# Loading the first rows per head pair, and ordering the first batch's steps by kind, in a fused attention and expert kernel

## The chip, the cores and the metric

The kernel runs on one core of one Trainium2 chip. The time is device microseconds of one execution. The kernel before was timed three times: 359.33, 359.04 and 358.71, median 359.04 us. One further execution was profiled.

In the text PE is TensorE (matmul, with PEld its weight load), DVE is VectorE, ACT is ScalarE, POOL is GpSimd, and SP is SyncE, which here only issues transfers.

## The reference

Attention over 4 batches, 8 heads, 768 positions, head size 64, with 4 sink positions and a window of 128; then a mixture of 4 experts over all 3072 tokens.

```python
scores = scale * q @ k.T
keep = (pos_k < 4) | (0 <= pos_q - pos_k < 128)
a = softmax(where(keep, scores, -1e9))
x = (a @ v) as [3072, 512]
p = domain_probs / domain_probs.sum(-1)
out = sum over e of p[:, e] * (relu(x @ w1[e]) @ w2[e])   # w1: 512x1024, w2: 1024x512
```

## The kernel before, in words

**Tiling.** A batch has 768 tokens, cut into three groups of 256 (g = 0, 1, 2; written (b, g)). Two heads make a head pair (hp 0 to 3), because two times 64 columns fill 128 partitions. For a group and a head pair the steps are: q and k rows are turned (`transposes`, lines 581 to 625, on TensorE for batch 0) and copied to `qkT`; `scores` (687 to 758) multiplies k by q into two PSUM banks, ScalarE takes the exponential into `aT` (line 746), VectorE multiplies the mask (line 754); `values` (763 to 830) multiplies by v, whose 65th column of ones gives the row sums, VectorE takes the reciprocal `R` (813) and multiplies (816, batch 0) or ScalarE does (825, later batches) into `onat`; `turn` (840 to 858) transposes that to `xT`, the input of the experts. In group 0 the mask is instead added on TensorE as a bias of -32768 before the scores (line 700). Groups 1 and 2 also use the sinks (`sinks`, 658), whose keys and values GpSimd prepares (lines 630 and 645).

**Experts.** For groups 0 and 1 of batch 0 the first layer of expert 0 is done directly (`emit_first`, line 1106, four pieces called hps of eight matmuls for a group and an expert), and so is that of (0, 2). Everything after, in `emit_fast` (1189, called cps), uses seven half-size products with sums of weights (`vf`, `qkn`, lines 404 to 410) and of tokens (`T`, line 1158) formed on VectorE. The second layer of groups (0, 0) and (0, 1) is direct (`emit_second`, 1433), of all others again in seven products (`emit_product`, 1358). Gates are applied in the first layer's eviction (lines 1223, 1131) from tiles that SP loads (485) out of a table in DRAM that `gates_by_row` writes (461 to 470).

**Transfers.** q and k of the first 256 rows of batch 0 come unconverted through SP and ScalarE's queue (`load_first`, 287) into `raw` tiles, and are converted by casts on VectorE and ScalarE (`cast_first`, 308). All other rows, v and the weights come through GpSimd, which converts in the transfer, one after the other in one queue: v blocks 0 and 1, then q and k rows of group 1 (`load_nat(0, 2)` and `(0, 3)`), v block 2, the first quarter of w1 of expert 0, v block 3, the other three quarters, w2 of expert 0 (lines 521 to 531), then what the loop adds.

**What sets the order.** Nothing is scheduled by the hardware: each engine runs its instructions in the order in which the program issues them. A planner at build time picks that order. It keeps a clock for each engine (`t`), adds an assumed duration for each instruction, and holds for every tile the time when it should be there. Its main loop (1494 to 1568) asks all possible TensorE steps for the time when they could run and a rank, and takes the lowest rank of those that are ready. Where nothing is ready for 220 ns it emits a filler product of 256 columns (`idle_products`, line 574). Work on ScalarE and VectorE is put on a list by `later(engine, ready, slack, run)`; when an engine's clock is free, `flush` takes, of the entries that are ready, the one with the smallest ready + slack. A small slack is thus a high rank. "any" lets the sooner of the two engines take it. The constants at the head of the kernel (60 to 113) are these ranks, shares and delays. `SHARE_OF` and `LEAD` pace the attention of the later batches against the experts' work, `GROW` is the earliest planner time (in ns) for `gates_by_row`.

Of the kernel before, what the change touches and what calls it, by code (L numbers as in the profile page):

```python
# [8 lines left out]
AF = mybir.ActivationFunctionType  # L9
# [7 lines left out]
def kernel(  # L17
# [20 lines left out]
    P = 128  # L38
# [19 lines left out]
    ]  # L58

    NGATE = 5  # L60
    START = {0: (1, 0), 1: (0, 1), 2: (0, 0), 3: (0, 0)}
    DENSE = 2
    NT3 = 3
    MIX = 4
    SHARE_OF = (0.634, 1.111, 1.102)
    LEAD = (1.272, 0.235)
    DUE = 0
    LOW_PRODUCT = 2.791
    LOW_SECOND = 4.402
    HIGH_PRODUCT = 0.207  # L70
    EARLY = 0.154
    GATE = 8921
    GATE0 = 5401
    FORM = 20576
    FORM2 = 37391
    TOKEN00 = 33179
    TOKEN0 = 1119
    WAIT2 = 16164
    WAIT1 = 5898
    LATE3 = 3  # L80
    TOKEN = 11155
    MARGIN = 494
    FULL = 7
    STEP0 = 0.141
    READY = 46
    WIDE = 2
    OPEN = 1.198
    ONACT = 1
    ONE = 2
    PAIR = 1  # L90
    SINK2 = 1
    PAD = 198
    MASKD = 99999999
    GROW = 24662
    ONLY2 = 1
    BEHIND = 7198
    CHORES = 2
    OWN = 2
    BIASED = 1
# [11 lines left out]
    FLIP = 421  # L111
    LATE = 259
    LATE1 = 12449

# [83 lines left out]
    def clock(engine, cols, rate=0.96, fixed=157):  # L198
        return act(cols) if engine == "act" else dve(cols, rate=rate, fixed=fixed)
# [86 lines left out]

    def load_first():

        raw = {name: mo.tile([P, 2, 4, 2 * D], FP32, name=f"{name}raw", tag=f"wide{i}", bufs=1) for i, name in enumerate("qk")}
        for half in range(2):  # L290
            hs = slice(4 * half, 4 * half + 4)
            for name, src in (("q", q), ("k", k)):
                x = raw[name][:, half]
                (nc.sync if name == "q" else nc.scalar).dma_start(
                    out=x, in_=src[0, hs, 0:G, :].rearrange("h (p t) d -> p h (t d)", t=2),
                )
                nat[0, half, name, "raw"] = x
            landed["first", half] = ((4870.0, 5180.0), (7550.0, 7350.0))[half]
            t["sp"] += 530

    def copy(engine, out, in_):
# [3 lines left out]
    qkn_free[-2:] = [1e12] * 2  # L305
    cast_at = {}

    def cast_first(half):
        hs = slice(4 * half, 4 * half + 4)

        def cast(at):
            cast_at[half] = at

        part = join(2, cast)
        for i, name in enumerate("qk"):
            def run(engine, i=i, name=name):
                copy(
                    engine, first[name][:, :, hs, :],
                    nat[0, half, name, "raw"].rearrange("p h (t d) -> p t h d", t=2),
                )  # L320
                part(clock(engine, 512))
            later(("dve", "act")[i], landed["first", half][i], 0, run)

    def rows_at(b, g):
        return max(landed.get(("qk", b, tb), 1e12) for tb in (2 * g, 2 * g + 1))
# [194 lines left out]
        pool(0, fixed=190)  # L520
    load_v(0, (0, 1))
    t["sw"] += 500
    for tb in (2, 3):
        load_nat(0, tb)
    load_v(0, (2,))
    load_w1(0, 4, [0])
    load_v(0, (3,))
    for i in range(1, 4):
        load_w1(0, 4, [i])
    t["sw"] += 700  # L530
    load_w2(0)

# [5 lines left out]
    low = [lent[:, 5 * P:8 * P], lent[:, 8 * P:10 * P]]  # L538
    nc.vector.tensor_scalar(
        out=low[0].rearrange("p (n q) -> p n q", n=3)[:, 0::2], in0=two, scalar1=LOW, scalar2=-LOW, op0=ALU.mult, op1=ALU.add,  # L540
    )
    nc.vector.tensor_scalar(out=low[0][:, P:2 * P], in0=own, scalar1=-LOW, scalar2=None, op0=ALU.mult)
    nc.vector.memset(low[0][0:NSINK, 0:2 * P], 0.0)
    nc.scalar.activation(out=low[1][:, 0:P], in_=own, func=AF.Copy, scale=-LOW)
    nc.scalar.activation(out=low[1][:, P:2 * P], in_=own, func=AF.Copy, scale=LOW, bias=-LOW)
    mask0 = consts.tile([P, 3 * P], BF16, name="mask0")
    mask1 = consts.tile([P, 2 * P], BF16, name="mask1")
    t["dve"] = t["act"] = 4600.0
    cast_first(0)
    flush(4700.0)  # L550
    for x in vx:
        nc.vector.memset(x[:, :, D:DX], 1.0)
    t["dve"] += 240.0
# [5 lines left out]
    nc.vector.memset(half, 0.0)  # L559
    for ph in range(2):  # L560
        nc.vector.memset(half[64 * ph:64 * ph + 64, ph:ph + 1], 1.0)
    for x in ksd:
        nc.vector.memset(x, 0.0)
    for x, y in zip((mask0, mask1), low):
        nc.vector.tensor_scalar(out=x, in0=y, scalar1=1 / LOW, scalar2=1.0, op0=ALU.mult, op1=ALU.add)
    t["dve"] += 400.0
    cast_first(1)

    acc = [psum.tile([P, 2 * G], FP32, name=f"acc{i}", tag=f"o{i}", bufs=1) for i in range(2)]

# [10 lines left out]
    def transposes(b, g, hp):  # L581

        if b not in qkT:
            qkT[b] = sb.tile([P, 2, NHP, S], BF16, name="qkT", tag="qkT", bufs=1)
        ready = max(cast_at[hp // 2] if (b, g) == (0, 0) else rows_at(b, g), free_at(2 if (b, g) == (0, 0) else 1))
# [6 lines left out]
        for i in range(2):  # L592
            for tt in range(2):
                if (b, g) == (0, 0):
                    nc.tensor.transpose(trs[i][:, i, tt], first["qk"[i]][:, tt, hs], ident)
                    continue
# [90 lines left out]
    def scores(b, hp, g, more=False):  # L687
# [4 lines left out]
        for ph in range(2):  # L692
# [4 lines left out]
        biased = b == 0 and g < BIASED  # L697
        if biased:
            for ph in range(2):
                nc.tensor.matmul(sps[ph][:, 0:w], lhsT=ident, rhs=low[min(g, 1)], start=True, stop=False, skip_group_check=True)  # L700
            pe(2 * w, ready, n=2)
        c = 0
        for (kb, qb, nq) in GROUPS[g]:
# [40 lines left out]
        for ph in range(2):  # L744
            def run(engine, ph=ph):
# [6 lines left out]
                def mask_one(engine):  # L752
                    x = a[:, ph].rearrange("p (n w) -> p n w", n=2)
                    nc.vector.tensor_mul(x, x, m[:, None, :].to_broadcast([P, 2, 2 * P]))
                    part(dve(w, rate=1.92))
                later("dve", at, 300, mask_one)
            later("act", done, 300 + 10 * ph, run)
        aTs[b, hp, g] = a

    def scores_ready(b, hp, g, n=1):  # L760
# [2 lines left out]
    def values(b, hp, g):  # L763
# [47 lines left out]
        def run(engine):  # L811
            R = sb.tile([P, 2, 2, 1], FP32, name="R", tag="R", bufs=6)
            nc.vector.reciprocal(out=R, in_=od[:, :, :, D:DX])  # L813
            at = dve(4, fixed=171)
            if b < ONACT:
                nc.vector.tensor_mul(  # L816
                    o[:, :, hp].rearrange("p q (h d) -> p q h d", h=2), od[:, :, :, 0:D], R.to_broadcast([P, 2, 2, D]),
                )
                scaled(dve(2 * P))
                return  # L820

            def multiply(engine):
# [17 lines left out]
    def turn(b, hp, g):  # L840
# [12 lines left out]
        def run(engine):  # L853
# [9 lines left out]
    class Attention:  # L863
# [23 lines left out]

        def flip_ready(self):
            _, b, g, hp = self.flips[0]
            rows = cast_at.get(hp // 2, 1e12) if (b, g) == (0, 0) else rows_at(b, g)  # L890
# [82 lines left out]
    class Mixture:  # L973


        def __init__(self):
            self.early = {g: list(range(E)) for g in range(DENSE)}
            self.open = []
            self.units = []
# [90 lines left out]
        def emit_first(self, what, ready):  # L1070
# [45 lines left out]
            if (b, g) not in PAIRS:  # L1116
                def run(engine):
# [343 lines left out]

    idle_products(acc[1], 9)
    mix = Mixture()
    att = Attention(0)
    work = [
# [137 lines left out]
```

## Time and profile before

| | |
|---|---|
| median of three runs | 359.04 us |
| profiled execution | 358.95 us, span 357.2 us, granted clock 1.00 |
| PE busy | 348.8 us, 98% |
| VectorE busy | 306.7 us, 86% |
| ScalarE busy | 168.7 us, 47% |
| GpSimd busy | 70.5 us, 20% |
| GpSimd's transfer queue | 17.31 MB, 55.4% of 16 transfer engines' span |

How to read it: the span runs from the first to the last instruction on the core. A line of a timeline or a chain gives start, duration, engine, source line, and written tile <- read tile. "[1.19 <-DMA kraw]" means that the engine sat idle for 1.19 us before it and that a transfer of kraw ended the wait. A busy share of PE is not work done: a matmul is pipelined, and its record holds its way through the array as well. Filler products count as busy.

### The profile page before, as it was taken

How to read it: one execution, taken by the hardware profiler on the slowest of the kernel's cores; microseconds unless marked ns; L12 is line 12 of the kernel's file. 1: busy time of each engine (PE TensorE's matmuls, PEld its weight loads, DVE VectorE, ACT ScalarE, POOL GpSimd, SP SyncE). 2: the span in 40 equal slices, each digit the busy share in tenths (PEclk: the TensorE clock that was granted, in tenths of full speed). 3: DMA queues.
4: the chain of work that ended last, by engine and by line, in shares of the span. 5: the costliest groups of instructions: out<-in, count | busy, mean ns of one | idle time of the engine just before them, and what ended most of it. 6: DMA issues, size and time to landing. Idle time of an engine off the chain costs nothing.

```text
span 357.2 us, 11108 instructions
## 1 busy us (share of the span) xinstructions
PE 348.8 (98%) x4673; PEld 302.6 (85%) x4673; DVE 306.7 (86%) x701; ACT 168.7 (47%) x432; POOL 70.5 (20%) x90
## 2 busy tenths in 40 slices
PE   8999999999999999999999999999999999999995
PEld 3675687777688998998998998899899999999884
DVE  6669999998799899899699799699799699999630
ACT  5866451437882922566444722926443632322110
POOL 8934114311260440420030620000000000000000
PEclk9999999999999999999999999999999999999999
DMA  9999999999993999691086999124112221100011
GB/s 175 185 195 203 230 210 174 137 135 139 227 148 42 138 168 157 75 119 46 32 68 111 148 156 139 50 54 55 44 32 63 59 52 51 37 31 31 1 61 60
DMA packets 115318, 37.86 MB, mean 106 GB/s; under 512 B 97196, under 2 KB 110764, under 8 KB 115268
## 3 DMA queue, kind: packets, MB, share of 16 engines
q0 software_dynamic: 74416, 17.31, 55.4%
q1 hardware_dynamic: 39796, 19.32, 29.3%
q8 instruction: 36, 0.59, 0.7%
q10 hardware_dynamic: 1056, 0.52, 0.6%
q14 instruction: 14, 0.11, 0.1%
HBM read 41.03 MB, written 6.34 MB: 133 GB/s over the span
## 4 chain that ended last, share of the span: by engine, by line
PE 83%; DVE 6%; ACT 5%; DMA 2%; issue 1%; POOL 1%; DVEq 0%
PE cps L1189 35%; PE acc L1358 31%; PE acc L1433 7%; PE hps L1106 3%; PE sps L706 3%; ACT onat L825 2%; PE od L786 2%; ACT aT L746 2%; DMA vx<-in_v_dram 2%; DVE H L1223 1%; DVE cps L1239 1%; DMA gates<-gate_rows 1%; PE od L779 1%; DVE onat L816 1%; DVE H L1254 1%
## 5 line engine op out<-in xcount | busy, mean ns | idle before, releaser
L1189 PEld LDWEIGHTS <-w 128*128 128x128 bf16 x1408 | 87.1, 98 | 3.5 <-issue 1.0
L1358 PEld LDWEIGHTS <-H 128*128 128x128 bf16 x720 | 66.6, 98 | 7.9 <-issue 1.2
L1223 DVE SCALAR_TENSOR_TENSOR H<-cps,gates 128x512 bf16<-128x512 f32 x105 | 69.8, 683 | 0.0
L1358 PE MATMUL acc<-w,H 128*128 128x256 bf16 x432 | 56.8, 273 | 0.1
L1189 PE MATMUL cps<-xT,w 128*128 128x128 bf16 x704 | 52.5, 219 | 0.5 <-ACT onat L825 0.5
L1189 PE MATMUL cps<-T,w 128*128 128x128 bf16 x704 | 52.5, 219 | 0.1
L746 ACT ACTIVATE aT<-sps 128x512 bf16<-128x512 f32 (+1 forms) x96 | 46.5, 571 | 9.7 <-PE sps L706 9.5
L1232 ACT COPY cps<-cps 128x512 f32<-128x512 f32 x44 | 25.7, 592 | 44.2 <-PE cps L1189 33.8
L1405 ACT COPY osb<-acc 128x256 f32<-128x256 f32 x40 | 15.4, 384 | 59.2 <-PE acc L1358 59.2
L825 ACT ACTIVATE onat<-od,R 128x64 bf16<-128x64 f32 x144 | 32.8, 349 | 21.7 <-DVE R L813 21.7
L1358 PE MATMUL acc<-wf,H 128*128 128x256 bf16 x288 | 39.3, 273 | 0.0
L1189 PEld LDWEIGHTS <-qkn 128*128 128x128 bf16 x576 | 34.8, 98 | 1.1 <-issue 0.2
L1239 DVE TENSOR_TENSOR cps<-H,cps 128x512 f32<-128x512 f32 x40 | 27.7, 691 | 9.0 <-PE cps L1189 6.2
L1358 PEld LDWEIGHTS <-S 128*128 128x128 bf16 x320 | 30.2, 98 | 4.2 <-issue 1.0
L1245 ACT COPY H<-cps 128x512 f32<-128x512 f32 x40 | 23.7, 600 | 18.1 <-PE cps L1189 18.1
L1433 PE MATMUL acc<-w,H 128*128 128x512 bf16 x128 | 30.1, 379 | 0.0
L1189 PEld LDWEIGHTS <-vf 128*128 128x128 bf16 x480 | 28.8, 98 | 0.1
L331 POOL DMA_DIRECT2D vx<-in_v_dram x24 | 21.4, 909 | 37.4 <-PE od L786 25.9
L1254 DVE TENSOR_TENSOR H<-H,cps 128x512 f32<-128x512 f32 x40 | 27.0, 680 | 1.7 <-PE cps L1189 1.6
L271 POOL DMA_DIRECT2D rows<-in_q_dram x18 | 16.0, 887 | 61.1 <-DMA qkT<-rows 51.0
L1189 PE MATMUL cps<-T,qkn 128*128 128x128 bf16 x384 | 27.3, 219 | 0.1
L727 DVE TENSOR_TENSOR aT<-aT,mask 128x1024 bf16<-128x1024 bf16 (+1 forms) x36 | 22.8, 641 | 1.9 <-ACT aT L746 1.6
(123 smaller groups left out, 524.2 us busy)
## 6 DMA issues: line engine op xcount, KB each, us to landing
w<-in_moe_w_dram POOLq DMA_DIRECT2D x7, 1024.0 KB, 23.1
out_dram<-osb SPq DMA_DIRECT2D x23, 256.0 KB
gates<-gate_rows SPq DMA_DIRECT2D x40, 128.0 KB
vx<-in_v_dram POOLq DMA_DIRECT2D x24, 128.0 KB, 10.0
rows<-in_q_dram POOLq DMA_DIRECT2D x18, 128.0 KB, 6.4
rows<-in_k_dram POOLq DMA_DIRECT2D x18, 128.0 KB, 6.7
w<-in_moe_w_dram POOLq DMA_DIRECT2D x4, 256.0 KB, 8.4
kraw<-in_k_dram ACTq DMA_DIRECT2D x2, 256.0 KB
```

The costliest lines, as they stand in the source:

```text
L331: nc.gpsimd.dma_start(out=vx[tb][:, :, 0:D], in_=v[b, :, tb * P:(tb + 1) * P, :].rearrange("h p d -> p h d"),)
L727: nc.vector.tensor_mul(x, x, m[:, None, :].to_broadcast([P, n, 2 * w // n]))
L746: nc.scalar.activation(out=a[:, ph], in_=sps[ph][:, 0:w], func=AF.Exp, scale=scale)
L825: nc.scalar.mul(o[:, qi, hp, ph * D:(ph + 1) * D], od[:, qi, ph, 0:D], R[:, qi, ph])
L1189: nc.tensor.matmul(y[:, f], lhsT=A[:, d, f * P:(f + 1) * P], rhs=T[:, d], start=(m in ("P1", "P5") and f == 0 and d == 0), stop=(d == 1), ...
L1223: nc.vector.scalar_tensor_tensor(out=dst, in0=src, scalar=0.0, in1=gate, op0=ALU.max, op1=ALU.mult)
L1232: nc.scalar.copy(out=tiles["Y"], in_=y)
L1239: nc.vector.tensor_add(tiles["V"], c5, tiles["X"])
L1245: nc.scalar.copy(out=c5, in_=y)
L1254: nc.vector.tensor_add(c5, c5, y)
L1358: nc.tensor.matmul(x, lhsT=self.operand(b, g, e, m)[:, f], rhs=forms[e][m][:, f], start=(k == 0 and f == 0 and m in (("P1", "P5", "P2") if ...
L1433: nc.tensor.matmul(op, lhsT=H[:, fb // QF, fb % QF, s], rhs=w2_sb[e][:, fb, :], start=(fb == 0), stop=(fb == NFB - 1),)
```

## The change: what it does

1. The first rows of q and k are loaded per head pair (four transfers of 128 KB each) instead of per four heads (two of 256 KB). k of head pairs 0 to 2 goes on ScalarE's queue, the other five on SP's. They are cast per head pair: k of pairs 0 and 1 on ScalarE, the other six on VectorE.
2. GpSimd's queue takes group 1's k rows before its q rows, and the first quarter of w1 of expert 0 before v block 2.
3. In batch 0, the slack of each kind of step is a constant of its own: exponentials 562, masks 1574, reciprocals 1728, turn copies 2154, evictions of hps 221 (the first eight with an engine given by a list), normalisation on ScalarE 269. Before they were 300, 300, 500, 200 and 400. Normalisation of head pairs 0 and 3 of group 0 and head pair 0 of group 1 moves to ScalarE.
4. Clearing and mask instructions of VectorE at the start go on the planner's list. The second mask is made from `own` in two instructions instead of from a second bias tile, which is dropped with its two ScalarE instructions.
5. Nine fillers of 512 columns at the start become four. Many constants of the planner have other values, `GROW` among them (24662 becomes 35000).

```diff
-    SHARE_OF = (0.634, 1.111, 1.102)
-    LEAD = (1.272, 0.235)
+    SHARE_OF = (0.61, 1.111, 1.102)
+    LEAD = (1.272, 0.328)
...
-    GROW = 24662
+    GROW = 35000
...
+    FIRST = (3500.0, 4500.0, 5500.0, 7200.0)
+    CAST = (("dve", "act"), ("dve", "act"), ("dve", "dve"), ("dve", "dve"))
+    BEGIN = (3450.0, 3600.0)
+    CLEAR = 1000
+    EARLY0 = (("n", 3), ("n", 2), ("w", 0), ("v", 2), ("v", 3), ("w", 1), ("w", 2), ("w", 3))
+    ACT0 = (0, 3)
+    ACT1 = (0,)
+    HPS0 = ("dve", "act", "any", "any", "dve", "dve", "act", "any")
+    S_MASK = 1574
+    S_VAL = 1728
+    S_TURN = 2154
+    S_HPS = 221
+    S_EXP = 562
+    S_MUL = 269
+    NACT = 3
+    NIDLE = 4
...
-        for half in range(2):
-            hs = slice(4 * half, 4 * half + 4)
+        for hp in range(NHP):
             for name, src in (("q", q), ("k", k)):
-                x = raw[name][:, half]
-                (nc.sync if name == "q" else nc.scalar).dma_start(
+                x = raw[name][:, hp]
+                (nc.scalar if name == "k" and hp < NACT else nc.sync).dma_start(
...
-                part(clock(engine, 512))
-            later(("dve", "act")[i], landed["first", half][i], 0, run)
+                part(clock(engine, 256))
+            later(CAST[hp][i], FIRST[hp], 100 * hp, run)
...
-    for tb in (2, 3):
-        load_nat(0, tb)
-    load_v(0, (2,))
-    load_w1(0, 4, [0])
-    load_v(0, (3,))
-    for i in range(1, 4):
-        load_w1(0, 4, [i])
+    for kind, i in EARLY0:
...
-    nc.scalar.activation(out=low[1][:, 0:P], in_=own, func=AF.Copy, scale=-LOW)
-    nc.scalar.activation(out=low[1][:, P:2 * P], in_=own, func=AF.Copy, scale=LOW, bias=-LOW)
...
+        nc.vector.tensor_scalar(out=mask1[:, 0:P], in0=own, scalar1=-1.0, scalar2=1.0, op0=ALU.mult, op1=ALU.add)
+        nc.vector.tensor_copy(out=mask1[:, P:2 * P], in_=own)
...
-                later("dve", at, 300, mask_one)
-            later("act", done, 300 + 10 * ph, run)
+                later("dve", at, S_MASK, mask_one)
+            later("act", done, (300 if b else S_EXP) + 10 * ph, run)
...
-            if b < ONACT:
+            if b < ONACT and hp not in ((ACT0, ACT1, ())[g]):
...
-            later("act", at, 600, multiply)
-        later("dve", done, 500, run)
+            later("act", at, 600 if b else S_MUL, multiply)
+        later("dve", done, 500 if b else S_VAL, run)
...
-        later("any", done, 200, run)
+        later("any", done, S_TURN, run)
...
-                later("any", end, 400, run)
+                later(HPS0[self.nhps] if self.nhps < len(HPS0) else "any", end, S_HPS, run)
+                self.nhps += 1
...
-    idle_products(acc[1], 9)
+    idle_products(acc[1], NIDLE)
```

More of the change, by code (lines that the diff above doesn't have):

```diff
@@ L60 @@
     NGATE = 5
+    FIRST = (3500.0, 4500.0, 5500.0, 7200.0)
[3 more added lines that the diff above has]
+    EARLY0 = (("n", 3), ("n", 2), ("w", 0), ("v", 2), ("v", 3), ("w", 1), ("w", 2), ("w", 3))
+    BIAS1 = ()
+    ACT0 = (0, 3)
[9 more added lines that the diff above has]
+    NIDLE = 4
     START = {0: (1, 0), 1: (0, 1), 2: (0, 0), 3: (0, 0)}
@@ L64 @@
     MIX = 4
-    SHARE_OF = (0.634, 1.111, 1.102)
-    LEAD = (1.272, 0.235)
+    SHARE_OF = (0.61, 1.111, 1.102)
+    LEAD = (1.272, 0.328)
     DUE = 0
[L68 to L79, printed above, removed]
+    LOW_PRODUCT = 2.872
+    LOW_SECOND = 4.475
+    HIGH_PRODUCT = 0
+    EARLY = 0.272
+    GATE = 9087
+    GATE0 = 5108
+    FORM = 22227
+    FORM2 = 45355
+    TOKEN00 = 28000
+    TOKEN0 = 1500
+    WAIT2 = 16819
+    WAIT1 = 5930
     LATE3 = 3
-    TOKEN = 11155
-    MARGIN = 494
+    TOKEN = 12447
+    MARGIN = 500
     FULL = 7
-    STEP0 = 0.141
-    READY = 46
+    STEP0 = 0.281
+    READY = 200
     WIDE = 2
-    OPEN = 1.198
+    OPEN = 0.991
     ONACT = 1
@@ L93 @@
     MASKD = 99999999
-    GROW = 24662
+    GROW = 35000
     ONLY2 = 1
-    BEHIND = 7198
+    BEHIND = 7891
     CHORES = 2
@@ L110 @@
     WARM = 6600.0
-    FLIP = 421
+    FLIP = 200
     LATE = 259
@@ L287, in load_first @@
     def load_first():
-        raw = {name: mo.tile([P, 2, 4, 2 * D], FP32, name=f"{name}raw", tag=f"wide{i}", bufs=1) for i, name in enumerate("qk")}
-        for half in range(2):
-            hs = slice(4 * half, 4 * half + 4)
+        raw = {name: mo.tile([P, NHP, 4 * D], FP32, name=f"{name}raw", tag=f"wide{i}", bufs=1) for i, name in enumerate("qk")}
+        for hp in range(NHP):
             for name, src in (("q", q), ("k", k)):
-                x = raw[name][:, half]
-                (nc.sync if name == "q" else nc.scalar).dma_start(
-                    out=x, in_=src[0, hs, 0:G, :].rearrange("h (p t) d -> p h (t d)", t=2),
-                )
-                nat[0, half, name, "raw"] = x
-            landed["first", half] = ((4870.0, 5180.0), (7550.0, 7350.0))[half]
+                x = raw[name][:, hp]
+                (nc.scalar if name == "k" and hp < NACT else nc.sync).dma_start(
+                    out=x.rearrange("p (h c) -> p h c", h=2),
+                    in_=src[0, 2 * hp:2 * hp + 2, 0:G, :].rearrange("h (p t) d -> p h (t d)", t=2),
+                )
+                nat[0, hp, name, "raw"] = x
             t["sp"] += 530
@@ L306, with cast_first, run @@
     cast_at = {}
-    def cast_first(half):
-        hs = slice(4 * half, 4 * half + 4)
+    def cast_first(hp):
         def cast(at):
-            cast_at[half] = at
+            cast_at[hp] = at
         part = join(2, cast)
         for i, name in enumerate("qk"):
-            def run(engine, i=i, name=name):
+            def run(engine, name=name):
                 copy(
-                    engine, first[name][:, :, hs, :],
-                    nat[0, half, name, "raw"].rearrange("p h (t d) -> p t h d", t=2),
-                )
-                part(clock(engine, 512))
-            later(("dve", "act")[i], landed["first", half][i], 0, run)
+                    engine, first[name][:, :, 2 * hp:2 * hp + 2],
+                    nat[0, hp, name, "raw"].rearrange("p (h t d) -> p t h d", h=2, t=2),
+                )
+                part(clock(engine, 256))
+            later(CAST[hp][i], FIRST[hp], 100 * hp, run)
     def rows_at(b, g):
@@ L522 @@
     t["sw"] += 500
-    for tb in (2, 3):
-        load_nat(0, tb)
-    load_v(0, (2,))
-    load_w1(0, 4, [0])
-    load_v(0, (3,))
-    for i in range(1, 4):
-        load_w1(0, 4, [i])
+    for kind, i in EARLY0:
+        if kind == "n":
+            load_nat(0, i)
+        elif kind == "v":
+            load_v(0, (i,))
+        else:
+            load_w1(0, 4, [i])
     t["sw"] += 700
@@ L537 @@
     LOW = 32768.0
-    low = [lent[:, 5 * P:8 * P], lent[:, 8 * P:10 * P]]
+    low = lent[:, 5 * P:8 * P]
     nc.vector.tensor_scalar(
-        out=low[0].rearrange("p (n q) -> p n q", n=3)[:, 0::2], in0=two, scalar1=LOW, scalar2=-LOW, op0=ALU.mult, op1=ALU.add,
+        out=low.rearrange("p (n q) -> p n q", n=3)[:, 0::2], in0=two, scalar1=LOW, scalar2=-LOW, op0=ALU.mult, op1=ALU.add,
     )
-    nc.vector.tensor_scalar(out=low[0][:, P:2 * P], in0=own, scalar1=-LOW, scalar2=None, op0=ALU.mult)
-    nc.vector.memset(low[0][0:NSINK, 0:2 * P], 0.0)
-    nc.scalar.activation(out=low[1][:, 0:P], in_=own, func=AF.Copy, scale=-LOW)
-    nc.scalar.activation(out=low[1][:, P:2 * P], in_=own, func=AF.Copy, scale=LOW, bias=-LOW)
+    nc.vector.tensor_scalar(out=low[:, P:2 * P], in0=own, scalar1=-LOW, scalar2=None, op0=ALU.mult)
+    if BIAS1:
+        low1 = lent[:, 8 * P:10 * P]
+        nc.vector.tensor_copy(out=low1[:, 0:P], in_=low[:, P:2 * P])
+        nc.vector.tensor_copy(out=low1[:, P:2 * P], in_=low[:, 2 * P:3 * P])
+    nc.vector.memset(low[0:NSINK, 0:2 * P], 0.0)
     mask0 = consts.tile([P, 3 * P], BF16, name="mask0")
     mask1 = consts.tile([P, 2 * P], BF16, name="mask1")
-    t["dve"] = t["act"] = 4600.0
-    cast_first(0)
-    flush(4700.0)
     for x in vx:
         nc.vector.memset(x[:, :, D:DX], 1.0)
-    t["dve"] += 240.0
     vsd = {}
@@ L557, with clear, masks @@
     ksd = [consts.tile([P, NHP, 32], BF16, name=f"ksd{i}") for i in range(2)]
[L559 to L567, printed above, removed]
+    t["dve"], t["act"] = BEGIN
+    for hp in range(NHP):
+        cast_first(hp)
+    def clear(engine):
+        nc.vector.memset(half, 0.0)
+        for ph in range(2):
+            nc.vector.memset(half[64 * ph:64 * ph + 64, ph:ph + 1], 1.0)
+        for x in ksd:
+            nc.vector.memset(x, 0.0)
+        t["dve"] += 400.0
+    def masks(engine):
+        nc.vector.tensor_scalar(out=mask0, in0=low, scalar1=1 / LOW, scalar2=1.0, op0=ALU.mult, op1=ALU.add)
+        nc.vector.tensor_scalar(out=mask1[:, 0:P], in0=own, scalar1=-1.0, scalar2=1.0, op0=ALU.mult, op1=ALU.add)
+        nc.vector.tensor_copy(out=mask1[:, P:2 * P], in_=own)
+        t["dve"] += 500.0
+    later("dve", 3600.0, CLEAR, clear)
+    later("dve", 3600.0, CLEAR + 300, masks)
     acc = [psum.tile([P, 2 * G], FP32, name=f"acc{i}", tag=f"o{i}", bufs=1) for i in range(2)]
@@ L584, in transposes @@
             qkT[b] = sb.tile([P, 2, NHP, S], BF16, name="qkT", tag="qkT", bufs=1)
-        ready = max(cast_at[hp // 2] if (b, g) == (0, 0) else rows_at(b, g), free_at(2 if (b, g) == (0, 0) else 1))
+        ready = max(cast_at[hp] if (b, g) == (0, 0) else rows_at(b, g), free_at(2 if (b, g) == (0, 0) else 1))
         slots, trs = [], []
@@ L592, in transposes @@
         for i in range(2):
+            if (b, g) == (0, 0):
+                for tt in range(2):
+                    nc.tensor.transpose(trs[i][:, i, tt], first["qk"[i]][:, tt, hs], ident)
+                continue
             for tt in range(2):
-                if (b, g) == (0, 0):
-                    nc.tensor.transpose(trs[i][:, i, tt], first["qk"[i]][:, tt, hs], ident)
-                    continue
                 for ph in range(2):
@@ L696, in scores @@
             ring[i] = 1e12
-        biased = b == 0 and g < BIASED
+        biased = b == 0 and (g < BIASED or g == 1 and hp in BIAS1)
         if biased:
             for ph in range(2):
-                nc.tensor.matmul(sps[ph][:, 0:w], lhsT=ident, rhs=low[min(g, 1)], start=True, stop=False, skip_group_check=True)
+                nc.tensor.matmul(
+                    sps[ph][:, 0:w].rearrange("p (n w) -> p n w", w=3 * P if g == 0 else 2 * P), lhsT=ident,
+                    rhs=low[:, None, :] if g == 0 else low1[:, None, :].to_broadcast([P, 2, 2 * P]),
+                    start=True, stop=False, skip_group_check=True,
+                )
             pe(2 * w, ready, n=2)
@@ L889, in flip_ready @@
             _, b, g, hp = self.flips[0]
-            rows = cast_at.get(hp // 2, 1e12) if (b, g) == (0, 0) else rows_at(b, g)
+            rows = cast_at.get(hp, 1e12) if (b, g) == (0, 0) else rows_at(b, g)
             return max(rows, free_at(2 if (b, g) == (0, 0) else 1), scored_at.get(b - 1, 0.0))
@@ L976, in __init__ @@
         def __init__(self):
+            self.nhps = 0
             self.early = {g: list(range(E)) for g in range(DENSE)}
```

## The prediction

> **What bounds the kernel now.** I read the page's busy totals first, then the busy time by stage, then the chain that ended last over the first 60 us, then the landings of the early transfers. TensorE (PE) is called 98% busy, but a matmul's record holds its pipeline latency, so I counted work instead: 104 matmuls of 128 columns take 5.81 us in the chain, 55.9 ns each, and eight of 512 columns take 1.73 us, 216 ns each. Both are columns / 2.4 GHz + 2.5 ns. Summed that way over all matmuls (a pair that uses 64 rows each counted once, four that use 32 columns each counted once, the filler products of line 574 left out) the useful work is 338 us. The span is 357.2, so 19 us are not work, and I placed them with the same sum over windows: 5.0 us from 0 to 5, 2.5 from 5 to 10, 1.5 from 10 to 13, 1.1 from 13 to 20, 1.1 from 20 to 25, 1.1 from 25 to 33: 12.3 in all before 33 us. From 33 to 354 only 3.6 are lost (2.2 of them between 80 and 120), and the end takes 3.7. So the kernel is bound by TensorE work after 33 us, and by the start before it. This change is mostly in the start.
>
> The busy time by stage; columns are busy time of PE, weight load, VectorE (DVE), ScalarE (ACT), GpSimd (POOL), granted clock, DMA share and GB/s:
>
> ```profile
> 5.00:10.00 5.00, 4.56 (x47) 2.57 (x45) 2.32 (x7) 3.88 (x10) 5.00 (x7) 1.00 1.97 193
> 20.00:25.00 5.00, 4.15 (x53) 3.41 (x50) 3.58 (x14) 2.54 (x5) 0.51 (x1) 1.00 1.42 199
> 30.00:40.00 10.00, 9.73 (x116) 5.88 (x111) 9.54 (x29) 6.49 (x14) 2.03 (x3) 1.00 1.20 219
> 40.00:50.00 10.00, 10.00 (x113) 7.83 (x112) 9.11 (x17) 5.09 (x10) 1.75 (x2) 1.00 1.17 218
> 60.00:80.00 20.00, 19.93 (x263) 15.93 (x261) 19.90 (x37) 8.85 (x16) 6.95 (x8) 1.00 1.81 140
> 100.00:120.00 20.00, 19.25 (x286) 17.24 (x284) 19.86 (x52) 11.64 (x37) 3.99 (x5) 1.00 1.11 90
> ```
>
> The reader should see a PE that has room until 25 us, and a VectorE that is nearly full from 30 us on. The chain, over the start:
>
> ```profile
> 3.52 5.80 DMA vx<-in_v_dram
> 12.03 0.55 PE acc L574 x5
> 15.22 1.58 ACT aT L746 x3
> 22.77 0.30 PE tx L847 x2
> 23.09 0.38 ACT xT L302
> 23.52 2.45 PE hps L1106 x21
> 25.97 0.60 PE acc L956 x4
> 31.33 1.83 PE acc L1433 x8
> ```
>
> The first thing the kernel waits for at length is not q or k but the second block of v, landed at 3.52 + 5.80 = 9.32. Then filler at 12.03, then group 1's exponentials and normalisation up to 23.46, then three first-layer pieces (hps), then the second layer (line 1433). The transfers issued by GpSimd go through one queue in order; issue plus time to landing, the first of these lines issued at 7.11 and the second at 10.94:
>
> ```profile
> w<-in_moe_w_dram POOLq DMA_DIRECT2D x1, 256.0 KB, 7.5
> w<-in_moe_w_dram POOLq DMA_DIRECT2D x1, 1024.0 KB, 14.0
> ```
>
> So expert 0's first quarter of w1 lands at 14.6 and its w2 at 24.9. In the same way group 1's q rows land at 10.4, its k rows at 12.1, v block 2 at 13.2, v block 3 at 15.5, the other quarters at 16.7, 18.4 and 19.5. Last, the first rows:
>
> ```profile
> 4.48 0.43 DVE L302 CAST qkn<-qraw 128x512 bf16<-128x512 f32 x1
> 4.93 0.62 ACT L302 CAST qkn<-kraw 128x512 bf16<-128x512 f32 x1 [1.19 <-DMA kraw<-in_k_dram]
> 5.72 0.54 PEld L595 LDWEIGHTS <-qkn 128*128 128x128 bf16 x8
> ```
>
> The first transposes come 0.17 us after ScalarE's cast ends, and that cast waited for k.
>
> **First rows per head pair.** The bytes stay; four transfers of 128 KB replace two of 256 KB per tensor. Counting packets of ScalarE's queue in half microseconds (16, 144, 244, 124, 74, 213, 232 from 2.5 to 6.0), its first 528 packets, one 256 KB transfer with its completions, are through at 4.5; the cast began 0.43 later. Half of them, 264, are through at about 3.7, so k of head pair 0 can be cast at about 4.15. A ScalarE copy of 128x256 takes 0.37 to 0.41 here; half the present cast is 0.31; I take 0.40, and 4.15 + 0.40 + 0.17 puts the first transposes at 4.7, 1.0 earlier. Head pair 2 follows at about 6.4 instead of 7.77 (third transfer through near 5.45). Head pair 3 needs all bytes (done at 6.1, plus 0.43) and two VectorE casts: 7.4 to 8.0 instead of 8.12. One more k transfer on SP, and two more q, push SP's v-sink loads back by three issues of 0.5 us; GpSimd uses them at 13.92, so that is covered unless they slip by more than 5 us. A third issue on ScalarE puts its table load 0.55 later (1.94 to 2.5, end 3.8), still before 4.15; the two bias activations it loses (0.31 and 0.29) had waited for nothing. VectorE makes the second mask in two instructions (0.15 to 0.25 each) where it had half of a 0.71 pair: at most 0.2, in a stretch where it was idle 1.23 us.
>
> The Trainium skill, page "DMA: Bandwidth & Descriptors", section "Anatomy of one DMA", gives a SWDGE fit of about 2.0 us plus bytes/436 GB/s; these are not SWDGE transfers, but by it halving one saves an estimated 0.3 us only, k could be cast at 4.65, and the sum would be 358.2, 0.5 of the 1.2 being lost. The packets counted above decide for 4.15 and for 357.7.
>
> **What covers it.** Values need v at 9.32, and GpSimd's order ahead of it is untouched. So the second or so gained at the front is not gained at 9.32. What is gained is that the softmax of head pairs 2 and 3 is no longer behind it: today their exponentials end at 11.11 and 12.32. Then ScalarE's two casts (0.8), four copies (1.4) and eight exponentials (8 x 0.43 = 3.5) from 4.15 are 5.7, so 9.9; with head pair 3's transposes at 7.8, copies 0.65, scores 0.7 and two exponentials 0.9 it is 10.1 to 10.5. One normalisation moved to ScalarE ahead of them (four instructions, 0.84) makes it at most 11.3. Normalising the four pairs on two engines (VectorE 0.6 each, ScalarE 0.84 each) and one turn each (0.3 and 0.38) then ends group 0 near 13.1 against 14.32: 1.2 earlier.
>
> **First quarter of the weights ahead of v block 2.** One 128 KB v block is worth 1.1 us of the queue (12.1 to 13.2). So the quarter lands near 13.5, not 14.6, and v block 2 at 14.6. Values of group 1 need block 3 (15.5, unmoved), so block 2 costs nothing. Swapping q and k rows changes nothing either, both are needed.
>
> **Steps ordered by kind, and the second cap.** Group 1's transposes start at 13.00 and its k rows are there at 12.1: 0.9 of room, more if the order on ScalarE (full from 14 to 18) or VectorE (full from 18 to 22) gets better: one normalisation less on VectorE is 0.42, and first-layer evictions now ranked ahead free banks sooner. Lower bound 0.9 from the k rows if nothing gets shorter, none at all if the chain only swaps waits. Upper bound: w2 of expert 0 at 24.9. The three hps and the gate transposes end at 26.49 now, so no more than 1.5 can be won before PE has nothing left to do until 24.9. I take 1.2, what group 0 gains, nearer the upper end since 2.2 us of PE time are still idle between 13 and 25.
>
> **Does it stay.** From 33 to 80 PE loses nothing in the trace, and it kept four dense pieces of expert 0 (3.5 us, at 52 to 58) in hand, so a PE that comes 1.2 us early to 34.9 (w1 of expert 1) and 41.7 (its w2) has other work. The gate-row sums move from 22.63, idle VectorE, to 35 or later: 0.24 + 0.18 + 0.30 + 0.32 = 1.04 us in its full stretch. PE loses nothing there now, so I cost it at nothing; 1.04 is its upper bound. The renumbered ranks and paces reorder everything after 33. No row prices that: at best it takes back part of the 3.6 us lost there, at worst it loses as much again. I take zero, since nothing in the rows leans either way. The filler cut from nine to four costs nothing by itself: single fillers are still put in wherever a wait is foreseen.
>
> **Sum.** The profiled execution took 358.95 for a span of 357.2, 1.7 outside it, 0.1 below the median of 359.04. 358.95 - 1.2 = 357.75; I say 357.7.
>
> **Rivals.** *Hidden:* group 1's chain is bound by eight exponentials of 0.52 and VectorE's eight masks of 0.43 and four normalisations of 0.6, whatever comes before; then its last turn stays near 23.1 and nothing is won: 358.9. For it: ScalarE is busy 4.0 of 4.0 us from 14 to 18. Against: it starts only at 13.00 with data there at 12.1. Chance 0.10.
>
> *Cold array:* 512-column fillers follow each other by 0.43 us up to 5.2, twice the later pitch, so the array runs at half rate for the first four microseconds although the rows grant 1.00. With fewer fillers and a gap near 4.2 this could last to about 8.5. The work of group 0 up to the scores is 0.9 + 1.3 + 0.9 = 3.1 us at full rate, 6.2 at half: from 4.7 it ends at 10.9, not 9.4, and 0.9 of the 1.2 is lost: 358.6. Chance 0.05. The Trainium skill, "TensorE: Matmul & The Clock Gate", section "What's actually happening", says that it takes about 3.4 us of sustained activity in a free-running window; the trace's switch near 5.4, 4.0 after the first filler, agrees.
>
> *Slower, by the pacing of later batches:* attention of batch 1 runs beside expert work from 80 to 120 and costs 2.2 us there, with ScalarE's normalisations and exponentials in the chain (98.48 to 101.95, 120.90 to 123.4). Batches 2 and 3 lose 0.9 (160 to 200) and 0.7 (220 to 240). The new shares call batch 1's steps due 4% sooner, so more of them meet unready scores or a full VectorE. If each of the later two loses what batch 1 loses, that adds 1.3 + 1.5 = 2.8: 358.95 - 1.2 + 2.8 = 360.5. It decides when the loss after 33 us passes 3.6 + 1.2 + 0.7 = 5.5. For it: the present order loses only 1% there, so a new one has more ways down than up. Chance 0.28.
>
> **How the numbers follow.** Forecast 0.57, hidden 0.10, cold 0.05, slower 0.28. A measurement can tell about 0.2%, 0.7 us. The forecast's own range is 356.5 (1.5 won at the start and 1.0 of the 3.6 later) to 358.3. The time falls below 356.4 perhaps once in fourteen (a larger part of the 3.6), and the slower case reaches beyond 361 as often. So 356.4 to 361.0. Faster 0.57; same 0.15, hidden and cold; slower 0.28.
>
> **What would show it.** Right: first transposes at 4.5 to 5.0, all exponentials of group 0 by 11.3, the first hps by 14, group 1's last turn by 22.5, then either no gap or a short wait for w2 at 24.9, useful work at 33 us about 1.2 ahead. Wrong: first values of group 0 much later than 9.4, or a loss after 33 us above 5.

## The result, and the profile after

The changed kernel takes 360.44 us (median of 7, 359.72 to 362.76) against 358.80 for the kernel before (7 runs, 358.70 to 359.33): 1.0052 times as long, 95% interval 1.0029 to 1.0076. It was forecast to be faster, at 357.7. The profiled execution took 359.72 for a span of 358.0. It is the fastest of the seven, so what the others lose beyond it, 0.7 us at the median, is not in this trace.

PE's busy total is unchanged (348.8 us in both). The time by stage of the changed kernel, columns as in the prediction:

```profile
20.00:25.00 5.00, 4.94 (x57) 4.27 (x55) 3.52 (x11) 2.32 (x6) 1.35 (x2) 1.00 1.38 200
40.00:50.00 10.00, 9.57 (x108) 7.28 (x107) 9.79 (x23) 4.45 (x8) 1.75 (x2) 1.00 1.24 214
50.00:60.00 10.00, 8.78 (x87) 6.54 (x86) 8.74 (x15) 1.82 (x3) 1.92 (x3) 1.00 1.65 204
```

The last of these stages in the kernel before:

```profile
50.00:60.00 10.00, 10.00 (x107) 7.75 (x105) 10.00 (x18) 1.82 (x3) 2.69 (x4) 1.00 1.63 193
```

PE is busier than before from 20 to 25 us (4.94 of 5 against 4.15), and idle where it had not been: 0.4 from 40 to 50, 1.2 from 50 to 60, a stage that was full. The chain from 44 to 54 us of the changed kernel says why:

```profile
36.44 8.93 DMA gate_rows<-scratch
45.39 6.01 DMA gates<-gate_rows
51.50 0.06 DVE H L1253
52.11 0.69 DVE H L1284
52.84 0.61 PE cps L1219 x8
```

The table of gates leaves at 36.44, is in DRAM at 45.37, the first tile read back from it is there at 51.40, and only then can VectorE do the first gated eviction, for which PE waits. VectorE's waits of that stretch name it:

```profile
DVE H L1253 <- DMA gates<-gate_rows: 1.3, 1, 1.3
```

The kernel before issued the same table at 23.81, and its VectorE came to the first gated eviction at 50.24 without a wait:

```profile
50.24 0.68 DVE L1223 SCALAR_TENSOR_TENSOR H<-cps,gates 128x512 bf16<-128x512 f32 x1
```

The price of the transfer could have been read there, in the waits of SP's queue of the kernel before:

```profile
SPq L485 <- DMA gate_rows<-scratch: 9.1, 1, 9.1
```

The two traces can be set side by side because PE does the same 104 products in one piece. By PE's timeline they start at 46.23 before and at 46.15 after; the first of the first-layer pieces kept in hand begins at 52.04 before and at 53.28 after. The same items then follow 1.2 us later, up to the last ones compared (110.38 and 111.60, 125.96 and 127.18). So the changed kernel is 0.1 ahead at the products and 1.2 behind after them, and up to 127 us nothing in the later batches adds to it. At the end of the span it is 0.8 behind.

The start itself, changed kernel:

```profile
4.06 0.40 ACT L318 CAST qkn<-kraw 128x256 bf16<-128x256 f32 x1 [0.38 <-DMA kraw<-in_k_dram]
4.39 0.34 PEld L618 LDWEIGHTS <-qkn 128*128 128x128 bf16 x4 [0.52 <-DVE half L576]
6.70 0.29 DVE L318 CAST qkn<-qraw 128x256 bf16<-128x256 f32 x1 [0.79 <-DMA qraw<-in_q_dram]
7.65 0.34 PE L734 MATMUL sps<-qkT 64*128 64x256 bf16 x4 [0.57 <-DVE qkT L318]
8.38 0.35 DVE L318 CAST qkn<-kraw 128x256 bf16<-128x256 f32 x1 [0.48 <-DMA kraw<-in_k_dram]
15.40 1.05 PE L1135 MATMUL hps<-xT,w 128*128 128x256 bf16 x8
```

The first transposes come at 4.4, but q of head pair 2 lands at 6.7 and k of head pair 3 at 8.4. VectorE runs in order, so head pair 1's copy stands behind the casts that wait for them, and its scores come at 7.65. The first hps (a first-layer piece) is at 15.40, 0.3 later than before.

### The profile page after: what moved, and what is told of

Same layout as the page of the kernel before. It is cut to its first block, busy times and chain, and to the rows that moved or that the text cites. A ratio compares the mean times of both kernels' runs of the same rounds, so it can differ in the third digit from the quotient of the medians.

```text
span 358.0 us, 11123 instructions
## 1 busy us (share of the span) xinstructions
PE 348.8 (97%) x4667; PEld 302.5 (84%) x4676; DVE 308.2 (86%) x708; ACT 168.1 (47%) x437; POOL 68.7 (19%) x90
## 4 chain that ended last, share of the span: by engine, by line
PE 83%; ACT 6%; DMA 6%; DVE 3%; issue 1%; SPq 0%; DVEq 0%
PE cps L1219 36%; PE acc L1388 33%; PE acc L1463 5%; PE hps L1135 3%; PE sps L734 3%; ACT onat L853 3%; DMA gate_rows<-scratch 2%; PE od L814 2%; ACT aT L774 2%; DMA gates<-gate_rows 2%; DMA qraw<-in_q_dram 1%; PE od L807 1%; DVE osb L1473 1%; PE sinks L691 0%; DVE T L1188 0%
## 5 line engine op out<-in xcount | busy, mean ns | idle before, releaser
L853 ACT ACTIVATE onat<-od,R 128x64 bf16<-128x64 f32 x156 | 35.6, 348 | 22.3 <-DVE R L841 22.3
L1463 PE MATMUL acc<-w,H 128*128 128x512 bf16 x119 | 28.7, 379 | 0.6 <-issue 0.2
```

The source lines that it names most:

```text
L1463: nc.tensor.matmul(op, lhsT=H[:, fb // QF, fb % QF, s], rhs=w2_sb[e][:, fb, :], start=(fb == 0), stop=(fb == NFB - 1),)
```

## The experiments

The theory that these traces suggest, called G: the gate sums, moved from planner time 24.7 to 35 us, cost the time, by the late table (W) and by VectorE's 1.04 us in its full stretch (D). Rivals: the renumbered paces (P), and a slower start (S). Differences below are the median less the median of the kernel before that ran on the same chip; the changed kernel stands at +1.64 in that measure.

**1. The sums early, all else as changed.** The five instructions are issued at 24.7, while the planner still counts their time at 35, so that no other instruction moves.

```diff
             gated_rows.append(1)
+            gates_clock()               # the planner's clocks only
+        if not summed and now > 24662:
+            summed.append(1)
             gates_by_row()
```

> The changed kernel with only the four gate-sum instructions and their transfer issued at planner time 24.7 us, as before, and every other instruction in the order of the changed kernel. Theory G (the gate table is written too late, its transfer takes 8.9 us and the tiles 6.0 more, and VectorE waits for them at 51.5): the wait of 1.3 us before the first gated eviction goes, the PE wait of 1.2 us goes with it, and the time is 358.6 to 359.2, about that of the kernel before, with a smaller spread than the 359.7 to 362.8 of the changed kernel. Rival P (new paces and ranks make a worse order): 360.0 to 360.8, unchanged. Rival S (the start is slower than before): above 359.5.

Measured: 357.59 against 359.06, -1.47, ratio 0.9964 (0.9951 to 0.9977). Faster than expected, and faster than the kernel before: G stands, P and S fall. Its chain:

```profile
45.10 5.81 PE cps L1221 x104
50.90 0.87 PE hps L1137 x8
```

The products start 1.3 ahead of the kernel before (44.93 by PE's timeline), and nothing interrupts what follows: the first piece kept in hand begins at 50.74. Of the 2.5 us between this run and the changed kernel (358.0 less 355.5 of span), 1.2 is there when the products start and 1.3 more when they are done.

Not all of that 1.2 comes from the sums. Both kernels have one order up to 24.7 us, and yet the first hps begins at 14.85 here and at 15.40 in the changed kernel. In the six profiled executions with this same start (the changed kernel, this run, run 3, both runs under 4 and the last run under 8) it begins between 14.85 and 15.72. From the first second-layer product to the 104 products it is 18.95 here (25.98 to 44.93) and 19.63 in the changed kernel (26.52 to 46.15). So in these two traces the late sums cost 0.7 ahead of the products and 1.3 within them, 2.0 of the 2.5; the other 0.5 was there at the first hps.

The rest of the new order costs nothing that these traces show: from the first piece kept in hand to the end of the span it is 304.7 in the changed kernel, 304.8 here and 305.2 in the kernel before.

**2. The sums late in the kernel before.** The same edit with 35000 in the old source.

> The kernel before with only those five instructions issued at planner time 35 us, every other instruction in its old order. Theory G: gate tiles land near 51.4, first use is at 50.2, so VectorE waits about 1.2 us or more and the time is 1.0 to 1.8 longer, 359.9 to 360.6, with a wider spread. Rivals P and S: nothing but at most 1.0 us of VectorE work in its full stretch, which PE does not feel: 358.7 to 359.2.

Measured: 361.79 against 359.06, +2.73, ratio 1.0091 (1.0068 to 1.0114). More than expected, and not by the wait: in its trace VectorE waits for no gate tile, the first use having moved to 51.73. PE waits behind the sums instead:

```profile
35.05 0.25 DVE L462 TENSOR_REDUCE scratch<-scratch 128x24 f32<-128x96 f32 x1
...
35.97 0.33 DVE L465 TENSOR_TENSOR scratch<-scratch 128x96 f32<-128x96 f32 x1
...
37.51 0.42 DVE L818 TENSOR_TENSOR onat<-od,R 128x256 bf16<-128x256 f32 x1
```

```profile
37.99 0.28 PE L849 MATMUL tx<-ident,onat 128*128 128x128 bf16 x2 [0.80 <-DVE onat L818]
```

Two items ahead of PE's next turn were pushed back by the 1.2 us that the sums fill. The products start at 47.73, 1.5 behind the kernel before, and the distance is the same after them (53.53). This profiled execution took 363.68, 1.9 above the run's median, and has two more waits of 1.0 near 104 for masks; how the rest of the 2.73 comes about is not settled by it.

**3. VectorE's share alone.** As run 1, and the four instructions once more at 35, without the transfer.

```diff
+    def gates_clock():
+        gates_by_row(True)              # four instructions, no transfer
```

> The first run (sums and transfer early) with the four gate-sum instructions done a second time, without the transfer, at planner time 35 us: the 1.04 us on VectorE of the late sums alone. Theory D (VectorE's share: its full stretch passes the 1.04 us on to PE): 358.3 to 358.8, 0.7 to 1.1 above the first run's 357.6. Rival (PE has other work, as the prediction costed it): 357.4 to 357.9. Rival (VectorE's time is the whole loss): 360.0 or more.

Measured: 358.48 against 359.02, -0.54, 0.93 above run 1. D as expected. In its trace PE waits for a normalisation that VectorE, busy without a break since the sums, comes to late. The same turn waits 0.38 at 40.72 in the changed kernel, and not at all in run 1:

```profile
40.34 0.28 PE L879 MATMUL tx<-ident,onat 128*128 128x128 bf16 x2 [0.47 <-DVE onat L848]
```

From the first second-layer product to the 104 products it is 19.63 (26.14 to 45.77), the figure of the changed kernel.

**4. The late table alone.** A first try issued only the transfer at 35.

```diff
     def gates_clock():
+        nc.sync.dma_start(out=gate_rows..., in_=pn)
```

> The first run's early sums, but the transfer that writes the gate table issued at planner time 35 us: the late landing alone. Theory W (the wait of VectorE for the gate tiles near 51.4): with PE about 1.5 us further at that place than in the changed kernel, 359.2 to 360.2, 1.6 to 2.6 above the first run. Rival (the tiles would land in time): 357.4 to 357.9.

Measured: 357.71 against 359.02, -1.31. It says nothing on W: SP's queue was empty and sent it at 25.34. It repeats run 1, within 0.2; against this repeat, on the same chip, run 3 is 0.77 slower. So ScalarE was put between:

```diff
     def gates_clock():
+        nc.scalar.copy(out=pc, in_=pn)
+        nc.sync.dma_start(out=gate_rows..., in_=pc)
```

> The run that issued the transfer late on SP did not delay it: SP had nothing before it and sent it at 25.3. Here ScalarE copies the finished sums to another place at planner time 35 us, and the transfer takes them from there, so that it cannot leave before about 35. VectorE's sums stay early; ScalarE has 3 us free of 10 there. Theory W (gate tiles land near 50 to 51.5, VectorE needs the first at 48.9 here): VectorE waits 1.3 to 2.5, and the time is 359.0 to 360.2, 1.4 to 2.6 above the first run's 357.6. Rival (late landing costs nothing, VectorE's 1.04 us were all): 357.5 to 358.0.

Measured: 359.13 against 359.03, +0.10, 1.57 above run 1. Its chain:

```profile
35.60 9.09 DMA gate_rows<-scratch
44.71 5.86 DMA gates<-gate_rows
50.67 0.06 DVE H L1257
51.27 0.69 DVE H L1288
52.01 0.61 PE cps L1223 x8
```

The same 15 us as in the changed kernel, and the same place that waits: the time is as W expected. The wait itself is not: VectorE waits 0.9 here, where 1.3 to 2.5 was expected, and PE comes to its first piece kept in hand 6.80 after the products begin (45.65 to 52.45), 1.0 more than in run 1. By the medians D and W give 0.93 + 1.57 = 2.5 of the 3.1 between run 1 (-1.47) and the changed kernel (+1.64). The remaining 0.6 is not told apart; the intervals are about half a microsecond wide on either side for the runs and 0.8 for the changed kernel.

**5. Two transfers per tensor instead of four.** As run 1, q in two halves on SP, k in two on ScalarE's queue, casts per head pair.

```diff
+                if hp % 2 == 0:
+                    (nc.scalar if name == "k" else nc.sync).dma_start(
+                        out=raw[name][:, hp:hp + 2]..., in_=src[0, 2 * hp:2 * hp + 4, 0:G, :]...)
```

> As the first run, and the first rows come again in two transfers of 256 KB per tensor, q on SP and k on ScalarE's queue; casts stay per head pair. Theory L (four small transfers per tensor move slower and the last of them meets GpSimd's queue, so k of head pair 3 lands at 8.3 instead of near 6.7): first cast about 0.8 us later (4.9), but head pair 3's cast 1.3 earlier (7.0), the four head pairs of group 0 end 0.3 to 1.0 earlier, and the time is 0 to 0.6 below the first run. Rival: the split helps, as was forecast, since the first transposes come first: 0.3 to 0.8 above the first run. Rival: the start is hidden by v and by w2 of expert 0: within 0.2 of the first run.

Measured: 359.36 against 359.06, +0.30, 1.77 above run 1. Theory L falls: the split helps, by more than expected. Part of this is another thing, as PE's timeline of this run shows:

```profile
4.86 0.39 PE L620 MATMUL tr<-ident,qkn 128*128 128x128 bf16 x2 [0.50 <-DVE half L578]
5.42 0.40 PE L620 MATMUL tr<-ident,qkn 128*128 128x128 bf16 x2 [0.17 <-ACT qkn L318]
6.73 0.85 PE L726 MATMUL sps<-lent,ident 128*128 128x384 bf16 x2
8.69 0.50 PE L736 MATMUL sps<-qkT 64*128 64x256 bf16 x4
10.56 0.49 PE L726 MATMUL sps<-lent,ident 128*128 128x384 bf16 x2
```

The same pair of bias products takes 0.85 at 6.7 and 0.49 at 10.6: the array runs at half rate for some 4 us longer (in run 1 the first pair, at 5.64, takes 0.54). The planner's fillers end at 4.4, and the first transposes now come at 4.86 and 5.42, with pauses before both. So the run was repeated with three more fillers:

```diff
     idle_products(acc[1], NIDLE)
+    for _ in range(3): nc.tensor.matmul(acc[1][:, 0:2 * G], lhsT=zeros..., rhs=zeros...)
```

> The run with two transfers of 256 KB per tensor, and three more fillers of 512 columns ahead of the first transposes, which keep PE busy from 4.2 to 5.4. Theory C (that run lost time because PE stood still from 4.2 to 5.4, the array then ran at half rate until about 10, as its bias pairs of 0.85 and its scores of 0.50 show against 0.49 and 0.34): full rate from about 5.5, and 358.2 to 358.8, between the first run and the run without the fillers. Rival (the later first cast alone is the loss): 359.2 to 359.6, no change. Rival (with the array at full rate two transfers are as good as four): 357.4 to 357.9.

Measured: 358.80 against 359.02, -0.22, 1.25 above run 1 and 0.5 below the run without these three fillers. Its pair at 6.93 takes 0.49, so the fillers do bring the full rate back. With PE fed the split is worth about 1.2 us, and these intervals lie apart (0.9985 to 1.0002 against 0.9951 to 0.9977). The 0.5 of the three fillers is not shown: the intervals overlap, and the run without them spread from 358.35 to 361.18, with a profiled execution 1.3 above its median. Nor is it shown where the 1.25 arises: the first hps of the run with fillers is at 15.68, within the 14.85 to 15.72 of the executions with four transfers. All three runs keep the order that was planned for four transfers; an order planned for two was not tried.

**6. The order by kind undone.** As run 1, with the old slacks, no normalisation of batch 0 on ScalarE, no engine list.

```diff
-    S_MASK = 1574; S_VAL = 1728; S_TURN = 2154; S_HPS = 221; S_EXP = 562; S_MUL = 269
+    S_MASK = 300;  S_VAL = 500;  S_TURN = 200;  S_HPS = 400; S_EXP = 300; S_MUL = 600
-    ACT0, ACT1 = (0, 3), (0,)
+    ACT0, ACT1 = (), ()
```

> The first run with the first batch's slacks as before (300, 300, 500, 200, 400, 600), no normalisation on ScalarE in batch 0 and no engine list for the first eight evictions; the planner makes the order from that. Theory K (ordering by kind is worth what the prediction gave groups 0 and 1 beyond the first cast, 0.5 to 1.0): 358.1 to 358.6. Rival (the gain of the first run is all from the first rows): 357.4 to 357.9.

Measured: 358.50 against 359.02, -0.52, 0.95 above run 1. The time is as theory K expected, at its upper end, but the trace does not show K's cause. After group 1 this run is hardly behind: its first second-layer product is at 26.30, against 25.98 in run 1, with the same eight hps done. It loses its time at the second layer of expert 1, first line below, where run 1, second line, does not wait:

```profile
42.77 3.61 PE L1465 MATMUL acc<-w,H 128*128 128x512 bf16 x15 [0.95 <-DMA w<-in_moe_w_dram]
41.48 3.62 PE L1465 MATMUL acc<-w,H 128*128 128x512 bf16 x15
```

This is a cap of the kind that the prediction looked for, one expert later. PE comes to it at 41.8, 0.3 later than in run 1, but w2 of expert 1 lands at 42.7 here and is there by 41.5 in run 1. Whether the other order makes it land later, or this one execution, is not settled; so what the order by kind is worth in groups 0 and 1 stays open.

**7. GpSimd's queue in the old order.** As run 1, q before k, v block 2 before the first quarter.

```diff
-    EARLY0 = (("n", 3), ("n", 2), ("w", 0), ("v", 2), ("v", 3), ...)
+    EARLY0 = (("n", 2), ("n", 3), ("v", 2), ("w", 0), ("v", 3), ...)
```

> The first run with GpSimd's queue as before: q rows before k rows, v block 2 before the first quarter of w1; the planner's clocks follow. Theory (the prediction's: the quarter 1.1 later, but the first hps stands behind other PE work anyway): 357.4 to 358.2. Rival (the first hps waits for the quarter at 14.6): 0.4 to 0.8 above the first run.

Measured: 357.90 against 359.03, -1.13, 0.34 above run 1, with intervals that overlap (0.9956 to 0.9980). As the theory expected: the queue's new order is worth little or nothing.

**8. Two tries to better it.** k of head pair 3 on ScalarE's queue too (`NACT = 4`):

> The first run with k of head pair 3 on ScalarE's queue too (four transfers on each queue). Theory Q (the fifth transfer of SP's queue is the last to land, 7.8 to 8.3, and holds back head pair 3's cast): its cast 0.3 to 0.8 earlier, 0.2 to 0.6 below the first run. Rival (a fourth issue of 0.5 on ScalarE puts its table load and its first cast back by as much): 0.2 to 0.6 above. Rival (group 0 is bound by v and ScalarE by then): within 0.2.

Measured: 357.51 against 359.03, -1.52, the same as run 1. Its last cast of k starts at 7.2, that of run 1 at 7.9; nothing comes of it, as the last of the three alternatives has it. And token sums not before 33.2 us (`TOKEN00 = 33179`):

> As the first run, and token sums may start from planner time 33.2 us as before, not 28.0; the planner makes a new order from there. Theory T (the lead of 0.9 us that the changed kernel has at 26.5 shrinks to 0.25 at 46 because eight token sums, 2.2 us of VectorE, stand before group 2's copies and masks at 29.7 to 34): 0.3 to 0.6 below the first run. Rival: the lead is lost to something else, for example weight sums and output evictions: within 0.2 of the first run.

Measured: 358.10 against 359.06, -0.96, 0.5 above run 1, intervals overlapping. Theory T falls. The shrinking lead needs no token sums. At the first second-layer product the changed kernel is 0.84 ahead of the kernel before (one hps of 0.87 more done, 0.03 later) and 0.08 at the products; run 1, with the late sums gone, is 1.38 ahead and then 1.30.

The fastest versions are run 1 and its variant with `NACT = 4`: 357.5 to 357.7, 0.35% below the kernel before and 0.8% below the changed one.

## Why the prediction was wrong, point by point

- **The step that failed is the gate-row sums**, "I cost it at nothing; 1.04 is its upper bound". Moving them late cost 3.1 us by the medians (2.0 between the two traces). Two things were wrong with it. The bound counted the four VectorE instructions alone, and not the transfers that hang on them, 9 us to write the table and 6 to read it back, of which the trace before showed the first. With the issue and the second landing as the trace after has them, 36.4 + 9 + 6 = 51.4, against a first use at 50.2 less whatever PE would gain, is a wait of 1.2 or more. And the nothing rested on PE losing no time while VectorE was full. That was no slack: 1.04 us more on VectorE there cost 0.93 (run 3; 0.7 in its trace).
- **The gain was right in size.** Without the late sums the change gives -1.47 where -1.2 was forecast. First transposes at 4.4 (forecast 4.7). As the next point shows, the 1.2 was not won where the prediction put it, so the agreement is in part luck.
- **It was wrong in its path.** Head pair 3's rows were to land at 6.5 and land at 8.4 (by 7.9 in run 1). The last exponentials of group 0 end at 12.38 in the changed kernel, not by 11.3, and the first hps is at 15.40, not by 14. The gain appears later, in group 1: its last copy begins at 22.34, not 23.09, and PE has done eight hps at the first second-layer product (26.52) where it had done seven (26.49). In run 1 the first hps is 0.25 ahead of the kernel before, and the first second-layer product 1.38. From the first hps to that product the kernel before takes 11.39 for seven hps, and the changed kernel 11.12 for eight; with the old ranks (run 6) it is 10.96, with the old queue (run 7) 11.12, with two transfers (run 5) 11.13, each for eight. So none of these three alone gives that gain, and which part of the change does stays open.
- **The cap by w2 at 24.9** did not bind: PE came to it at 25.98 in run 1.
- **Two transfers instead of four** costs 1.25 with the array at full rate (run 5). The prediction took v at 9.32 as cover for the front, and put the gain into the softmax behind it. Four transfers are worth something, as it said; where that arises the traces do not show.
- **The cold-array rival** (5%) did not happen in the changed kernel, whose pair at 5.88 takes 0.49, but its mechanism did in the run with halves. The Trainium skill, page "TensorE: Matmul & The Clock Gate", section "What's actually happening", has the array reach full rate after a busy window of about 3.4 us, in windows that run free of the kernel's start. That run, fed from 1.4 to 4.4 and without a pause from 5.4, and at full rate only about 10, agrees. The rival's own sum was too high: with the half rate ending at 8.5, as it assumed, group 0's 3.1 us of work from 4.7 would end near 9.7, not 10.9.
- **The slower rival, the pacing of later batches** (28%), had the right sign and the wrong place: from 54 to 127 us the changed kernel keeps its distance to the kernel before, as above. That its 360.5 is near the measured 360.44 is a coincidence. The zero that the prediction took for the renumbered ranks and paces agrees with the traces after the products; no run tried them alone.

## What to carry to other kernels

When an instruction is moved to another time, follow it to the last consumer of what it starts: each transfer behind it at the landing time that the trace shows at that load, not the instruction alone. An engine that is busy without a break and on which nobody waits is not free: that it is never waited for may hold by a margin smaller than what is added, and adding the same work twice tells it in one run. A loss in one part of a change can hide a gain in another, so undo the suspect with every other instruction left in its place.

## What the runs showed of the hardware

A transfer of 48 KB from SP, written in runs of 96 bytes while GpSimd's queue was full of weights, took 8.9 us to land in the changed kernel and 9.1 in the second run under 4; in the kernel before SP waited 9.1 for it. In the changed kernel it was issued at 36.44, its queue moved no packet until 40, and then about 100 to 150 a microsecond until 44. The Trainium skill, page "DMA: Bandwidth & Descriptors", section "Anatomy of one DMA", puts the fixed cost at about 2.0 us, for transfers issued by GpSimd; by it the table would be there near 38.5, an estimate. The measurement, 45.37, decides. A tile of 128 KB read back right after took 6.0. Whether the load or the short runs make it so slow was not tried.
